# One half of an attention input loaded by a transposing DMA instead of being transposed on TensorE

## The chip, the cores and the metric

The kernel runs on one core of a Trainium2 chip. The core has TensorE (PE, matrix multiply into PSUM), VectorE (DVE), ScalarE (ACT), GpSimd (POOL) and SyncE (SP, which here only issues DMAs). A weight load of TensorE has its own row in the profile (PEld). The metric is device time in microseconds (us) from one execution; the kernel before takes 721.76 us (median of three runs, 721.74 to 721.97).

## The reference

Two independent problems, A and B, of the same shape; the outputs are joined along the last axis. For each, with 16 batches, 80 query rows, width 576, 32 query heads, 16 key/value heads, 512 cached positions and head size 128:

```
q = (x @ wq).reshape(B, Sq, 32, 128).transpose(0, 2, 1, 3)
k, v = repeat(k_cache, 2, axis=1), repeat(v_cache, 2, axis=1)
p = softmax(einsum("bhqd,bhkd->bhqk", q, k) * 128 ** -0.5)
o = einsum("bhqk,bhkd->bhqd", p, v)
out = o.transpose(0, 2, 1, 3).reshape(B, Sq, 4096) @ wo
```

All inputs and the output are bf16.

## The kernel before

**The pieces.** A unit U is one batch and four key/value heads (eight query heads), 64 units a problem, 128 in all. For each unit TensorE makes five score tiles of 128 x 512: four with the first 128 of the 160 query rows of a key head (L673, "S"), and one that gathers the four remainders of 32 rows (L660, "SR", issued for one or two units at a time). On each tile VectorE takes the negated row maximum (L682), ScalarE the exponential with its row sum (L686); VectorE inverts the sums in two groups (L692: tiles 0 to 2, tiles 3 and 4), and GpSimd multiplies the tile by them (L695, "norm"). Then TensorE transposes the five tiles in 40 small matmuls against the identity (L727, "T"), VectorE or ScalarE copies the result to pT (L738 to L747), TensorE multiplies with V (L770, "PV", four matmuls a key head) and VectorE or ScalarE copies to oT (L784). The output projection is L816 ("P", eight matmuls each), with its sums copied at L828 and L845 and stored at L851.

**The query projection** (L537, four matmuls over the first 512 of the 576 columns, "Q", and L550 for the last 64 columns, two matmuls that lie on opposite halves of the array) needs x transposed: `xT[128, half, 5, 640]`, where a half is 8 batches = 640 rows, chunks 0 to 3 hold columns 0 to 511 and chunk 4 holds columns 512 to 575 twice, once in each 64 partitions. Half 0 of problem A is needed first; half 1 from the query projections Q46 on, which stand at about 46 us. There are two ways to fill xT:

- Problem A, both halves: two plain DMAs a half (L375, three and two blocks of 128 rows) into `xs`, which lies in the accumulator `acc`. GpSimd doubles the last 64 columns (L383, two a half). For each block, TensorE does four 128 x 128 transposes into a PSUM bank (L396, "X") and VectorE one copy to xT (L401). For the last columns TensorE does three and two more (L414, "X2"), with two VectorE copies (L418).
- Problem B, both halves: one transposing DMA a half writes chunks 0 to 3 of xT (L431), two small plain DMAs bring the last 64 columns into `xst` (L437, five blocks, and L436, the first block once more), TensorE transposes them in five matmuls (L451, "X2") and VectorE copies in three instructions (L456 to L458).

**Queues.** All DMAs are issued by SP in one order. A K load is a transposing DMA of 1 MB for two units (L626; six slots, so three pairs); a V load is 512 KB for one unit (L630); wo comes in pieces of 576 KB (L590), wq in pieces of 256 KB or 1 MB (L502) with its last 64 rows (L506).

**The order of the work** is written out by hand in a table, `ORDER`. Each operation belongs to a stream; the streams, sorted by name, are given the letters of `LETTERS`. Each letter in the table takes the next operation of its stream; the digits after it are the PSUM banks that it takes; an apostrophe ahead of it sends a copy to ScalarE instead of VectorE. Every engine runs its operations in the order of the table, and the waits follow from it: an operation waits for those whose results it reads and for the readers of what it overwrites. The numbers that are given with each operation (`k_`, `xk`, `XK`) only order operations inside a stream. Some letters: a K loads, h V loads, F wo, K x loads, d query projections, e S, f SR, g T, c PV, b P, j X, k X2, l and m exponentials, o and p maxima, C inverses, u and v norms, M and L the VectorE copies of X and X2.

Read off the table, SP issues at the start (x0 to x3 are the four plain loads of x, K0 is the load for units 0 and 1):

```
x0 x1, wq (12 pieces), K0 x2 K1 x3 V0 V1 K2 wo0 V2 K3 V3 wo1 K4 V4 V5 V6 K5 V7 V8 K6 V9 K7
```

and TensorE, around the transposes of half 1 (X5 to X9 are blocks of four, X22 and X23 the last columns of half 1; Qn with n up to 41 counts L537 groups and L550 pairs):

```
... S8 T0 S9 S10 X5 X6 Q36 X7 S11 Q37 S12 Q38 X22 Q39 X23 S13 PV0 PV1 S14 Q40 Q41 T1
S15 Q42 X8 S16 S17 X9 S18 PV2 PV3 PV4 PV5 SR3 Q43 PV6 PV7 T2 S19 Q44 S20 S21 Q45 T3 ...
```

Of the kernel before, what the change touches and what calls it, by code (L numbers as in the profile page):

```python
# [31 lines left out]
LQ = 12  # L32
QPO = 1
QO = 192
X2K = 6.0
# [8 lines left out]
XK = (15.0, 15.0)  # L44
# [21 lines left out]
omcpg07lCsuc4'yCze1e5'wvmcob7u'Aolue0te2'xe6olhud4hoblholae0Bd5lCove1f23'qolug67Cplud0wumzc1cpu'yc7e2'Axe6smcd
4o'BCg13olutle5uc2xCco'zue7c6'sBd3vlwoe2e4u'ycCod5'Aulhtc1e0huoclag67sloe1'zc2yc'xlCf47Coud6'tBv'wle0pe2c5uAcm
c1ouc'se3od4'tulpg15vlob0'wCyluxe2'zAue1bomhColaue6e7d3oluc5Be2'qocle0d4Colug16sluof57'zvyd2lCpc6u'wc'xp'Ae0uc
1md3Bo'tcmg45hF'se6'yxe1hCBc7u'zFe4oclae5vb3olute0lwboolc7Ce1olud6Acluc4qcCovd3se0ulg25Cou'tf17'yxuCBe4'zd2wvp
lc3d5uAmoe0ucpg16'sulob3wlze4A'ye6bhCouholavc2d1q'xulcd3tme0Bf26og45plpc7mcyd0'wme2sc4oc'ze7d6C'txulBc4cou'Ae5  # L70
c3'socle1g24o'thlChCe7uxb3'who'yua'Ae2le5uoe0b'zuolCe1Bd4ulod6vloc7ue2lCqcc5ovlcg03slCtvf17y'zue2'xCb3p'Buwmpc
6ucAbmuo'sue0le1hoc7ud4'qhold3hae2lcCovg56'tluf01y'zub7w'xCpu'Be2Ambuople0c3oc'qc4'se2d5loce7C'td3vole0ug46lub
2'zCymohb'wJxBGe1'qc7oJcle2hc3Ald4hoe0acClod5vsg16lu'tuf27C'zwyb3u'xpuc6AmcuBe0e1oe4uc5bsloc'qd6tle0od3oe1lg25
olCb4pu'zxmwue0ye5blvABd6oc7ohle1e2Jqd3lGochg04slJof57a'w'yAc1pcb6'tCCx'zvle0d4uo'Be1c2umocd3ule5buloCslug01Cp
'quc2w'x'ye6Aue5cmod4u'zte0d7o'Ble1og23loc6'wCcylud5az'sue2'Ac0xe6lCocuc3'BcCv'toc4e1lcuod7'tlsuf02lg34upmb6y'
zwhpe0'xd3'AaComue1e5c4Blvcoc2c'svod7lute0le4og12ole5bxz'ylCoe0ud2'w'BAc4ule1Cod3v'qhcolc7uhe6Chcloug05h'tsuhl
f17xauB'ye4e6p'wb3'zpmc5od0mocle1Ad7slg24CouCc6'yzvce5'xC'te2wvd4ole6oulboule1Bc5ulAce2oud7'qoc3ulcCsg06lu'tuf
15z'w'ye2pb3'x'Bhomc7hCAculae0e1od4ubplComuc6e0qd2luog35slCuf17x'yBc'wu'zpe0d3'tomc5cCpc6u'Ae2le1scvod4'tvog05
lhuhle6zb2a'yCoume1we0vod5'x'Bc7Aulcoc4cld3t'se6e1log47ole0bCCo'wulzud6'x'yBe1u'Ae7Coc4ld3uo'qe5hvclag02sulof1
4u'wxlAc7cp'yb6p't'ze0e7moe2c5cBlbCouod3lvCc1slue0qcd5omuhhf27tlug46pe0y'wb1'zC'xou'Be6mFbvolue2qc4'Ae5olcac3s  # L80
d1CCpcud4'toulg06vb3'wzluA'xue2me6Bboyld4oe1Fc7od5lhqg02lf36'wz'Ae1xcCoc4u'sce2Blhud7od5'tp'ye1Ke4lob0mCoue2bl
puolvg13lc4z'ycc2q'se1acmoe0e4b3xlCCou'td6Bulwd2ovg15AluCf07w'zCve4'ype5b'AuomFoue1lKc6xd0uKo'qe4lhd3uolcuBc5c
'se2ltg16aob5p'w'zClxuc4ce6u'se2obmCB'Aud4olve0Cc7lod3u'ycug26ltrf17'ywChxve0'zpc5h'AcuDoe2'Be6'sc4oumck3ohuc5
lctd1'sLle0c4d5loe2coalg36C'tud0w'zyue4'xd6'Bolg35AlCpuc2c'yze1vc4'w'xoe3'Ab5umolBe0coc7'te6e1lscCe4oule2baoul
oe0ld3Coud6'sClrug17oluCf45z'yvc2p'wc'xd7uA'tmc1Bucpe2lc3vFoce6mDud4thloe0hg35soe2'zb1o'x'yCwe5luBbColue6lrud3
oDd4luhe0'Ag12holaCf57luyc6z'wvc'x'Ae0pc1'sue2'Bcome6c3pd4lCcCou'td5moug01lsue7z'wc3'xuclBd2ov'Ae1'yd5olg46Ctu
lhf07zhv'ye3pc1'wud4'Aomce2pc6lcod0'shC'xe3tu'Bc1aocle6ub5Cslvome1uc3ocg27u'te3'yzbloe2lrb7ole1e6loe5e3bDolaCC
xlb2uo'Buod6'wluCAd1lruc4g05uf37uy'zc'xwvd5Bpe0bhpmDAc1csd3C'thrumCg46JouDlf12xuwBc7'yczue0e4sc3cpb7'thoGc3ole
6bolCAe0luce5sb4urvoDe7d3ovle6boalome0d5Crlpg14lb7wx'ACov'zc3e6ucoe4'tbu'yomuBc3crhluc5CDe1d7luoclsd2hCvlg36DJ
u'tf04y'w'Aue1'ze5oe7ue3b6Caolupbluomd5xr'Bc1olcd6Cpluc2cvg07tsue2zme1b3Gw'xC'yoJue7oKd4luc0Blcoe2c6'Ascle1oe5  # L90
d0'tolg67oCe2z'xbulov'w'Be1re7'Aud0lCod3ulyKg45uClohuf26Jw'yxKCe1'zupc4hc'ABuc5mae0pcvlc3ocud2ts'sle7d3ome5Cg1
4ovlc6ulxcwod0u'Be7A'yd3o'te1lzg26lCouf45'w'zxd7Aulpe6hc0'yDcoc1'Bacsme2Cc3puclc0ok4umctd6vC'sLe1lug35'toue4'z
e0ob2lo'ye5we1lCbxuBloue6e4'Aoc3lacd7olc5ocld0sC'te1rulg36ovf25'yzue4lpe3b6wmxpc1'Acoh'Bd2mhCCc7svDe0lochud5o'
te1lug47oluCe3xblyuo'zue0e1'wBd4luaod5'Aole7g23rlof06'wz'yc1'xCcp'Auc3le2Bcuc4C'sod5mupe1clue0Coc7mcvhsd2Dot't
ve4lDg67uhlohd3ux'yhze1e0'Bd6o'wlc7oe2lcAc4c'sCoe5ulhg17tulof04v'zCxb2p'wulyd7u'BAmc5pe1cc3msce0ohe6'td5oalg34
olCe1ub'zo'yvxle0wd3CuB'Arc4lucoe2c7uod5le1'scolg06tlCf24zu'yDe7pe1uhb6xamwvCobuplud2Cmrc7uoe0'Ae6c'BuCoc3lcuo
d4lsug15lCtvf07'x'yve6p'wb3'zuBhobuDAlFe1c4moce2e6lod5d0olc1rclDg23t'shpe1'ye6Cwb4umAxuze2'BboCoc7lucc3lsvd5rc
uoe0Dd4thlg67oaf12w'zCCub3'xp'Avyme7e5uobloule1rc6ulcod3Be0lc7Cocud4'tslCg15vhDe7u'zxb6ao'wu'ACyle0e5bpomd3r'B
c7oe1lcoc4'se2d6lCovcg07u'tluf45w'xy'zd1uF'Bpe0luhd7Ac6moucpg23'slc4ze6cob0yle3FbmoaC'tCe2xule6oe5b4uolure3'wb
louolvd2CBe0'Aud6qloug57f14z'x'Bc3y'wc'Ae7d6'sDold3hCplue2c5Ccomug07hplvc1t'xucC'zwe2c5'yuod7'Bcu'se0lthe3uc1o  # L100
ac'Ac5'socme2d6tloe1b4Cloue0lvg35oluby'zxlwe1Ce2uo'Bf35'Aoue0ld6qvFld7phc4ocmc2se1lcpg34htae0y'zb2'xC'w'BuAc3m
ocuc7'sCcolue6e5Cd3olvd4tluoe1g07uCole6vzb'xluo'Be7wud5'qCy'Ae1ulof24ud3plac6ocmg07Cslvpe2'zud6wx'yc1oue7mcAud
0o'te5lBg14olf23zlhc7xchp'Be4c5D'ywe0Ccs'Aud1mohc7uo'tcle2d5sole6g47Coluc0Cz'xuc'yd2ph'wvle7c4oauc'te6'Ac0luoc
b1t'Blse0d4moe7Cg56lovle3uwe0xbo'yuC'zoue7'Ae5qc6lucoc2le1CBcuad3o'slud4olg06tCluf27xCy'ze5ub1'Bpu'womc4ucCe0l
# [162 lines left out]
def bass_concat_heads__gqa_block_cached__gqa_block_cached__near_ridge_kernel(  # L267
# [27 lines left out]
    with ExitStack() as es:  # L295
# [634 lines left out]
```

## Time and profile before

| what | value |
|---|---|
| median of three runs | 721.76 us |
| the profiled execution, its time | 722.56 us |
| its span, first to last instruction | 720.6 us |
| TensorE busy | 715.3 us, 10820 matmuls |
| VectorE, ScalarE, GpSimd busy | 641.3, 639.8, 432.6 us |
| DMA queue of SP | 159.05 MB, 95.6% of 16 engines' span |
| granted TensorE clock | 1.000 |
| x of problem A: plain loads, median to landing | 4.1 us (432 KB), 3.7 us (288 KB) |
| x of problem B: transposing load, median to landing | 7.5 us |
| K loads of problem A: median to landing | 8.9 us |

The page gives busy time by engine, then the chain of work that ended last, then groups of instructions by source line. "Busy" of TensorE is made of intervals whose ends are modelled and that overlap; what one matmul costs in a row of equal ones is the distance between their starts, which the timeline shows. An entry of the waits names the engine that waited and what ended the wait.

### The profile page before, as it was taken

Reading aid. Unit: us, or ns where it says so; the run is one execution under the profiler, and the core shown is the slowest. Engines: PE = TensorE matmul, PEld = TensorE weight load, DVE = VectorE, ACT = ScalarE, POOL = GpSimd, SP = SyncE. Lnnn points to the kernel's source line nnn. Section 1 sums busy time; section 2 is a strip of 40 time slices with the busy share of each in tenths; the row PEclk is TensorE's granted clock in tenths of the full one; section 3 lists DMA queues with packets and bytes.
Section 4 is the critical chain, followed back from the end, with each engine's and each line's share of the span. In section 5 each row is a group of like instructions: output and inputs, shape, how many; then the busy total and the mean of one; then the engine's idle time right before and its main releaser. Section 6 shows DMA issues by size and latency. Waiting matters only on the chain.

```text
span 720.6 us, 26290 instructions
## 1 busy us (share of the span) xinstructions
PE 715.3 (99%) x10820; PEld 513.1 (71%) x10820; DVE 641.3 (89%) x1459; ACT 639.8 (89%) x1844; POOL 432.6 (60%) x650
## 2 busy tenths in 40 slices
PE   9999999999999999999999999999999999999998
PEld 5567767777677777777777777777777777777777
DVE  3999998899888998899998899979999889998995
ACT  1999999799989998789997899989999889998993
POOL 0477755566556675665675567646676656755773
PEclk9999999999999999999999999999999999999999
DMA  9999999899999999999999998999999898988860
GB/s 248 268 269 259 265 255 241 206 189 259 225 241 209 217 254 240 226 254 205 268 207 219 248 245 212 247 236 204 181 262 224 193 241 198 220 194 200 178 199 18
DMA packets 374167, 160.73 MB, mean 223 GB/s; under 512 B 278560, under 2 KB 370976, under 8 KB 374048
## 3 DMA queue, kind: packets, MB, share of 16 engines
q1 hardware_dynamic: 374048, 159.05, 95.6%
q8 instruction: 86, 1.41, 0.8%
q14 instruction: 33, 0.27, 0.1%
HBM read 87.65 MB, written 2.95 MB: 126 GB/s over the span
## 4 chain that ended last, share of the span: by engine, by line
PE 98%; ACT 1%; issue 0%; DVE 0%
PE ps L816 22%; PE ps L770 20%; PE ps L537 19%; PE ps L673 16%; PE ps L727 11%; PE ps L660 5%; PE ps L550 4%; ACT p_sb L686 1%; PE ps L348 0%; PE ps L396 0%; ACT qT L563 0%; PE ps L414 0%; PE ps L451 0%; DVE osb L845 0%; DVE wo_sb L341 0%
## 5 line engine op out<-in xcount | busy, mean ns | idle before, releaser
L695 POOL TENSOR_SCALAR p_sb<-p_sb,rinv 128x512 bf16<-128x512 bf16 x640 | 430.8, 694 | 272.7 <-DVE rinv L692 272.2
L686 ACT ACTIVATE p_sb<-ps,negmax 128x512 bf16<-128x512 f32 x640 | 444.0, 711 | 29.8 <-DVE negmax L682 25.5
L682 DVE TENSOR_REDUCE negmax<-ps 128x1 f32<-128x512 f32 x640 | 419.2, 681 | 27.5 <-PE ps L673 22.2
L770 PE MATMUL ps<-pT,v_sb 128*128 128x160 bf16 x2048 | 191.1, 233 | 0.1
L770 PEld LDWEIGHTS ps<-pT,v_sb 128*128 128x128 bf16 x2048 | 154.0, 98 | 39.5 <-ACT pT L745 3.3
L816 PE MATMUL ps<-wo_sb,oT 128*128 128x288 bf16 x1280 | 181.6, 286 | 0.0
L673 PE MATMUL ps<-kT,qT 128*128 128x512 bf16 x512 | 176.4, 381 | 0.0
L537 PE MATMUL ps<-xT,wq_sb 128*128 128x320 bf16 x1024 | 176.0, 299 | 0.0
L816 PEld LDWEIGHTS ps<-wo_sb,oT 128*128 128x128 bf16 x1280 | 122.1, 98 | 43.2 <-ACT p_sb L686 1.7
L686 ACT ACTIVATION_READ_ACCUMULATOR p_sb<-ps,negmax 128x1 f32 x640 | 144.0, 225 | 0.0
L537 PEld LDWEIGHTS ps<-xT,wq_sb 128*128 128x128 bf16 x1024 | 94.5, 98 | 42.4 <-ACT p_sb L686 2.2
L727 PEld LDWEIGHTS ps<-ident,p_sb 64*128 64x128 bf16 x5120 | 91.4, 95 | 8.8 <-issue 1.1
L727 PE MATMUL ps<-ident,p_sb 64*128 64x64 bf16 x5120 | 96.1, 190 | 1.2 <-ACT qT L563 0.7
L738 ACT COPY pT<-ps 128x512 f32<-128x512 f32 x150 | 88.4, 603 | 9.4 <-PE ps L727 9.0
L740 DVE COPY pT<-ps 128x1024 bf16<-128x1024 bf16 x106 | 72.0, 684 | 13.2 <-PE ps L727 11.7
L563 ACT ACTIVATE qT<-ps 128x320 bf16<-128x320 f32 x131 | 59.5, 462 | 16.2 <-PE ps L550 15.4
L784 DVE CAST oT<-ps 128x320 bf16<-128x320 f32 x129 | 61.5, 482 | 6.5 <-PE ps L770 6.0
L564 DVE TENSOR_SCALAR qT<-ps 128x320 bf16<-128x320 f32 x125 | 59.5, 482 | 8.1 <-PE ps L550 6.6
L673 PEld LDWEIGHTS ps<-kT,qT 128*128 128x128 bf16 x512 | 48.4, 97 | 25.7 <-issue 3.3
L784 ACT CAST oT<-ps 128x320 bf16<-128x320 f32 x127 | 56.4, 448 | 10.2 <-PE ps L770 9.9
L745 ACT COPY pT<-ps 128x128 f32<-128x128 f32 x132 | 36.1, 288 | 7.0 <-PE ps L727 6.8
L692 DVE RECIPROCAL rinv<-rowsum 128x3 f32<-128x3 f32 (+1 forms) x256 | 39.5, 161 | 2.3 <-ACT p_sb L686 2.2
(31 smaller groups left out, 194.7 us busy)
## 6 DMA issues: line engine op xcount, KB each, us to landing
v_sb<-in_A_v_cache_dram SPq DMA_DIRECT2D x64, 512.0 KB, 5.4
v_sb<-in_B_v_cache_dram SPq DMA_DIRECT2D x64, 512.0 KB, 4.9
wo_sb<-in_A_wo_dram SPq DMA_DIRECT2D x8, 576.0 KB, 5.6
wo_sb<-in_B_wo_dram SPq DMA_DIRECT2D x8, 576.0 KB, 5.6
wq_sb<-in_B_wq_dram SPq DMA_DIRECT2D x4, 1024.0 KB, 6.6
out_dram<-osb SPq DMA_DIRECT2D x40, 72.0 KB, 3.4
wq_sb<-in_A_wq_dram SPq DMA_DIRECT2D x8, 256.0 KB, 4.5
wq_sb<-in_A_wq_dram SPq DMA_DIRECT2D x2, 1024.0 KB, 7.3
```

Of the source, the lines that this page charges most:

```text
L537: last = e.matmul(ps[:, vbq[h].phys, QO:QO + 320], lhsT=wq_sb[:, wsl, ck, hi * 128:(hi + 1) * 128], rhs=xT[:, half, ck, n0:n0 + 320], star ...
L563: return e.activation(dst, src, AF.Identity, scale=SCALE)
L673: return e.matmul(ps[:, vb.phys, :], lhsT=qT[:, qsl, bl, gl * 160:gl * 160 + 128], rhs=k_of(U, gl), start=True, stop=True)
L682: return e.tensor_reduce(negmax[:, si:si + 1], ps[:, vb.phys, :], axis=AX.X, op=AluOpType.max, negate=True)
L686: return e.activation(p_sb[:, psl, :], ps[:, vb.phys, :], AF.Exp, bias=negmax[:, si:si + 1], scale=1.0, accum_out=rowsum[:, ss, k:k + 1])
L695: return e.tensor_scalar(p_sb[:, psl, :], p_sb[:, psl, :], rinv[:, ss, k:k + 1], 1.0, op0=AluOpType.mult, op1=AluOpType.mult)
L727: last = e.matmul(dst, lhsT=p_sb[64 * h:64 * h + 64, psls[k_], j * 128:(j + 1) * 128], rhs=ident[64 * h:64 * h + 64, 64 * h:64 * h + 64], ...
L738: return e.copy(pT[:, pts, :, :].bitcast(F32)[:, :, 32 * h:32 * h + 32], ps[:, vtp[h].phys, :].rearrange("p (n c) -> p n c", n=16))
L740: return e.tensor_copy(pT[:, pts, :, 64 * h:64 * h + 64], psb[:, vtp[h].phys, :].rearrange("p (n c) -> p n c", n=16))
L770: last = e.matmul(ps[:, vo.phys, off:off + 160], lhsT=v_sb[:, vs, gl, j * 128:(j + 1) * 128], rhs=pT[:, pts, 4 * gl + j, :], start=(j == 0 ...
L784: return (e.copy if en == "act" else e.tensor_copy)(dst, src)
L816: last = e.matmul(ps[:, vb.phys, 0:DC], lhsT=oT[:, sp_ * (HH // 2) + i, rb * 128:(rb + 1) * 128], rhs=wo_sb[:, 2 * c3 + sp_, i, :], start= ...
```

## The change

Half 1 of problem A is now loaded as the halves of problem B are. The first loop over halves runs over half 0 only; the second runs over three cases (problem, half): (0, 1), (1, 0), (1, 1). The table of the order is made anew; it has 13 operations fewer (two plain x loads, five X and two X2 groups of TensorE, five and two VectorE copies, two GpSimd copies go; three loads, one X2 group and one VectorE operation of three copies come).

```diff
-LETTERS = "abcdefghijklmnopqrstuvwxyzABCDEFGHIJKLMNO"
+LETTERS = "abcdefghijklmnopqrstuvwxyzABCDEFGHIJKLMN"
 ORDER = """
-nEKni7KHHHHHHNj3Ej4IMk5j6MNIj7j3Mk4ILd6Id5IIdd2AaBd1dd5BAd6dd2'Bd1dd6BMd0AdAd7'BAd5Ldd4'A'Bd6dd5'ABKMd7add3'AB
...
+nEKni7KHHHHHINj3j4HMj5k6MNIMk3j4ILd5Id6IIdd2BaAd1dj5Ad6Md2dd4ALd0BBdd3BMd6dd5'B'Ad2dd4BA'Ad6dad3BAd5dd4'ABEf0f
+1pe2e7d3omodle6e5Ad0loe2d4'BphldaCod3vmd6Bu'Aodle1uBd4'Aoe0le7Cd3ouldoe2lf56AC'Boe1ve0ld3puld4pumdouhmAhog2357
+lKCBud6'yze1lud4xo'we7g0235Colvdw'xuz'Be1c2lcouf05'As'ye7Cpe6luc3cpmue2c4ocK'te1mod0Kd3aole5ole7slCCg46ouloud2
+lCc1zv'ye5wue6xloe4cu'Aok7ld0vLh'tuc5lFcoe1Fug67holas'yCe4Buc5'wlCof36u'zcpe1u'te7xo'Bc5vcmAc0ucold2sd3lpe5log
+14Ctle7e0omb5ylod6xe1lCbvo'w'zuBe0lqd7uCoc3cuhg45'shulac3yu'Ad1'zCxcuw'Be0f25'tov'Ae7pe4uld3oumg06ploc2c'zxc7y
...
-        for half in range(NPP):
+        for half in range(1):
             x_ap = probs[0][0]
...
-        for half in range(NPP):
-            x_ap = probs[1][0]
+        for xp, half in ((0, 1), (1, 0), (1, 1)):
+            x_ap = probs[xp][0]
...
-            k_ = 5.0 * (UPR + 16 * half - LQ) - XK[half]
-            S.add("sp", k_, em_ldxt, writes=[R(("xT", half, b_), 1) for b_ in range(NRT)], dsem="d_x%d0" % half,
-                  name="ldxt%d" % half, stream="x")
+            k_ = 5.0 * (UPR * xp + 16 * half - LQ) - XK[half]
+            S.add("sp", k_, em_ldxt, writes=[R(("xT", half, b_), xp) for b_ in range(NRT)], dsem="d_x%d0" % half,
+                  name="ldxt%d.%d" % (xp, half), stream="x")
...
-            S.add("pe", k_ + X2K, em_xtr2, reads=[R(("xst", t), half) for t in range(2)] + [IDENT], writes=[R(vb, 0)],
-                  name="xtt%d" % half, stream="X2", alloc=[vb])
+            S.add("pe", k_ + X2K, em_xtr2, reads=[R(("xst", t), 2 * xp + half) for t in range(2)] + [IDENT], writes=[R(vb, 0)],
+                  name="xtt%d.%d" % (xp, half), stream="X2", alloc=[vb])
```

Read off the new table, SP's order at the start is

```
x0 x1, wq (12 pieces), K0 K1 V0 K2 V1 V2 x2 x3 x4 K3 V3 wo0 wo1 V4 K4 V5 V6 K5 V7 V8 K6 V9 wo2 K7
```

where x2 is the transposing load of half 1 and x3, x4 its two small ones, and TensorE's is

```
... SR0 SR1 S0 S1 Q25 Q26 S2 S3 ... S8 SR2 S9 S10 Q36 Q37 Q38 T0 Q39 S11 Q40 S12 T1 Q41 S13 PV0 PV1 SR3 S14 S15 PV2 PV3
S16 PV4 PV5 S17 Q42 Q43 S18 S19 T2 Q44 PV6 S20 S21 S22 PV7 X22 Q45 PV8 PV9 S23 T3 S24 PV10 SR4 PV11 S25 S26 PV12
PV13 PV14 PV15 Q46 Q47 S27 T4 S28 S29 P0 Q48 ... S32 SR5 S33 S34 Q51 T6 ...
```

where X22 is now the one group of five for the last columns of half 1 (the groups are numbered as they come; it is the third of them). Over the whole table the copies that go to ScalarE change: 68 instead of 56 and 72 instead of 71 of the two oT streams, 27 instead of 23 of the accumulator's, and within five of the old number for the pT and qT copies.

More of the change, by code (lines that the diff above doesn't have):

```diff
@@ L66 @@
[L66 to L80, printed above, removed]
@@ new lines @@
+xe1ob7'tole2FCe5Clobuhohuld3aqule0Cwe1od7v'A'Bof25ulg46pulpb0umw'ye1e2'xombAloe5c3'qcole1c4Cc'sue0'ztd2uold3ol
+g46BCe5'ywuc7hc'Ad4hvlshe1oe2u'xa'zc7CcCo'Bud0ltug36olvf57xlzud1'ypc6u'wc'BCAc3u'scpmd4vCe0'te2muog56oulc3xcu'
+we7lsd0o'yc3c'Be2e5'zob4lAhlte6ac1Ccoue7c3olcubt'sole1d3'qolg56f24'wxlzb7C'ypue1me6uoc5cbCBlhupa'suc3Ame1d5ov'
+qd2olve0Cclug47Co'tuf16lyvb3w'zCup'x'Be0Aubmoupe1lc7ucoh'qc4'se0hd3lohd5hlCe1Gvcog27J'tuJle0uyhb4'xmaoe1we2ob'
+AlCzud3loue0'qc7old6c'Bg14'slf27z'ye5p'xc0'Be1d4wmocc6o'Aclc3td2ple0cC'soug15tue6wmb3Coulze7ub'yov'xlBc5e0'qd2
@@ new lines @@
+loe1e6Clod3ucohlug07aA'se1y'wb4lCou'xc6Be0lubCz'Auoe1cvCd3ltvd5o'qe0lf27g46ppmb1Goh'x'Bc2zJclbay'swmCe0ve2oc4'
+qe7ucCold5utc6le1oucc4'Aoc'sud3lCtug26luf07'yxwuCe1'zpe2d4u'Bpmc3uco'Ad6v'soe0lg35ouluc1yhcld2Jz'te3h'xCe0we1u
+'Bhoc5mchoub6hlsvole7c5c'Ad3thlog04aClue1ze5b'yuCw'xo'Aue0o'qe7c4lvcoc6lue2Bce1old3Csd5'tulog46uolf07z'yb2x'wp
+'Alpc4e6e3'Bocmc1cCCsud5'told4ug01mulue6azb'w'xo'ye1Be7lc3Coe0u'Acod4'quld5ovle2sf16Colug37pub0'zCxauw'Bylbupm
+ve2c7mocc3qe1le6oce0'td5old7Colug12sluhf36z'yvhc0p'xhc'w'Ae1Chc2Amve4ocd5'Butld3ou'sg07Cplue1'ywud2o'ze0c4x'Aa
@@ new lines @@
+234r'zDf17x'ze2'wplb4pme0oe6mc5aCcCyuc1lbouole2vcoe7le3ub0o'tusle1rc6lboolg2457CCruDe3y'wDe0lue2cob5'zuColve1o
+blauColue0rc7'scCu'xlg2356tuof47'zwuc1lpcc6u'xye2mcvoe0'sc3c'toue1lc4ove6hclDb5Ctuh'sCplhug0234ohub'zwyu'xle0r
+vg1234moDf56'zwCc7'xuple1e2ocu'yc4e0Cmpb3uslvobmuolcre1hc7'toe6lDcg2345sloe0c7'ywe1o'zce2lb4tCoule7Cboulxuole0
+c3ruclc6oDe1v'sclg2457tCof36u'yCe0'zCpub5loume7we1uxboluolg0234vrlpc7Duc'wChc5z'yue0c'xCmsug1234o'tuc7'zye6c'w
+ulxc4ocve1'sc3tlcog0257'sc4'zxe6Cycv'wb7'toulbulc3Ccub5suc3g1246cy'zb'txwc3cc4scb6r'trDbDb7brDrD
@@ L437, in em_ldxs @@
                 return e.dma_start(xst[:, 0:NRT, :], src.rearrange("(k p) d -> p k d", p=128))
-            k_ = 5.0 * (UPR + 16 * half - LQ) - XK[half]
-            S.add("sp", k_, em_ldxt, writes=[R(("xT", half, b_), 1) for b_ in range(NRT)], dsem="d_x%d0" % half,
-                  name="ldxt%d" % half, stream="x")
+            k_ = 5.0 * (UPR * xp + 16 * half - LQ) - XK[half]
+            S.add("sp", k_, em_ldxt, writes=[R(("xT", half, b_), xp) for b_ in range(NRT)], dsem="d_x%d0" % half,
+                  name="ldxt%d.%d" % (xp, half), stream="x")
             for t in range(2):
-                S.add("sp", k_ + 0.01 + 0.01 * t, lambda e, t=t, f=em_ldxs: f(e, t), writes=[R(("xst", t), half)], dsem="d_xt",
-                      name="ldxs%d.%d" % (half, t), stream="x")
+                S.add("sp", k_ + 0.01 + 0.01 * t, lambda e, t=t, f=em_ldxs: f(e, t), writes=[R(("xst", t), 2 * xp + half)], dsem="d_xt",
+                      name="ldxs%d.%d.%d" % (xp, half, t), stream="x")
             vb = S.bank()
@@ L458, in em_xev2 @@
                 return e.tensor_copy(xT[64:128, half, 4, 0:128], psb[64:128, vb.phys, NROW - 128:NROW])
-            S.add("pe", k_ + X2K, em_xtr2, reads=[R(("xst", t), half) for t in range(2)] + [IDENT], writes=[R(vb, 0)],
-                  name="xtt%d" % half, stream="X2", alloc=[vb])
-            S.add("dve", k_ + X2K + 0.5, em_xev2, reads=[R(vb, 0)], writes=[R(("xt", half, b_), 1) for b_ in range(NRT)],
-                  name="xte%d" % half, stream="xe2")
+            S.add("pe", k_ + X2K, em_xtr2, reads=[R(("xst", t), 2 * xp + half) for t in range(2)] + [IDENT], writes=[R(vb, 0)],
+                  name="xtt%d.%d" % (xp, half), stream="X2", alloc=[vb])
+            S.add("dve", k_ + X2K + 0.5, em_xev2, reads=[R(vb, 0)], writes=[R(("xt", half, b_), xp) for b_ in range(NRT)],
+                  name="xte%d.%d" % (xp, half), stream="xe2")
         steps = [(g_, b_) for g_ in range(ILV) for b_ in range(8)]
```

98 lines of the change are left out of this document (47 added, 51 removed).

## The prediction

> **What bounds the kernel now.** I read the page first, its busy line and the chain that ended last; then the time by stage, to see whether the bound is the same everywhere; then TensorE's waits and its timeline where the removed transposes stand; last the DMA side. Busy line and chain:
>
> ```profile
> PE 715.3 (99%) x10820; PEld 513.1 (71%) x10820; DVE 641.3 (89%) x1459; ACT 639.8 (89%) x1844; POOL 432.6 (60%) x650
> PE 98%; ACT 1%; issue 0%; DVE 0%
> ```
>
> The chain is nearly all TensorE. By stage (stretch, length, then busy time of PE, PEld, DVE, ACT, POOL, the granted clock, the DMA engines' share, GB/s):
>
> ```profile
> 0.00:20.00 20.00, 18.76 (x125) 10.51 (x126) 7.42 (x20) 3.80 (x7) 1.32 (x8) 1.00 1.05 244
> 20.00:28.00 8.00, 7.52 (x54) 3.30 (x53) 8.00 (x17) 7.99 (x25) 3.38 (x6) 1.00 1.14 278
> 28.00:40.00 12.00, 11.82 (x180) 8.27 (x181) 11.91 (x30) 12.00 (x37) 8.12 (x14) 1.00 1.15 265
> 40.00:60.00 20.00, 20.00 (x353) 13.93 (x351) 19.98 (x47) 20.00 (x62) 14.11 (x22) 1.00 1.11 272
> 60.00:718.00 658.00, 657.24 (x10114) 477.08 (x10111) 593.52 (x1348) 596.05 (x1717) 405.71 (x603) 1.00 0.96 220
> ```
>
> After 60 us PE alone is full; from 20 to 60 us VectorE, ScalarE and the DMA engines are full as well, and this is where the change acts. PE's waits are small, the one at T0 in front:
>
> ```profile
> PE ps L348 <- DVE wo_sb L341: 1.2, 1, 1.2
> PE ps L727 <- ACT qT L563: 0.7, 1, 0.7
> ```
>
> PE's timeline at half 1 of A (start, duration, line, count):
>
> ```profile
> 29.40 0.61 PE L396 MATMUL ps<-ident,acc 128*128 128x128 bf16 x8
> 29.85 0.71 PE L537 MATMUL ps<-xT,wq_sb 128*128 128x320 bf16 x4
> ...
> 32.01 0.34 PE L414 MATMUL ps<-ident,acc 128*128 128x128 bf16 x3
> 32.24 0.72 PE L537 MATMUL ps<-xT,wq_sb 128*128 128x320 bf16 x4
> ```
>
> Eight transposes hold PE from 29.40 to 29.85: 0.45 us, 0.056 us each, though one is recorded at 0.219 us. SP's timeline shows how loaded the DMA side is there:
>
> ```profile
> 22.97 7.11 SPq L626 DMA_TRANSPOSE kT<-in_A_k_cache_dram  x1
> 30.20 0.51 SPq L590 DMA_DIRECT2D wo_sb<-in_A_wo_dram  x1
> 30.75 0.58 SPq L630 DMA_DIRECT2D v_sb<-in_A_v_cache_dram  x1
> 31.38 6.95 SPq L626 DMA_TRANSPOSE kT<-in_A_k_cache_dram  x1
> ```
>
> and the transposing loads of problem B's x, the nearest rows for the new one (shortest, median, longest in ns, then to landing):
>
> ```profile
> L431 SPq DMA_TRANSPOSE xT<-in_B_x_dram x2: 3182/4224/5265, 216.8 to 312.6; - x2
> DMA to landing us min/median/max: 7.3/7.5/7.6
> ```
>
> **TensorE's work.** The removed groups hold PE, by distances to the next start, for 0.45 (X5, X6), 0.26 (X7), 0.22 (X8) and 0.25 us (X9), and the last columns for 0.23 and 0.11: 1.52 us. The five added ones took 0.28 us twice in problem B (238.67 to 238.95, 332.00 to 332.28). Net -1.24. PE is the path there (its only wait near is T0's), so this counts in full. Against it, block 4 of half 0 (X4) stood before the first query projection, while PE waited for VectorE's copies (done at 6.71, Q0 at 6.76); the new order has it behind Q5, in the full stream: +0.22, or 0 if Q0 comes earlier by it.
>
> The TensorE page of the Trainium skill, "TensorE: Matmul & The Clock Gate" (Part 4), gives about 275 ns for such a transpose in a kernel. By that, 20 fewer would be an estimated 5.5 us. The timeline disagrees: 56 ns apart.
>
> **The other engines.** VectorE loses five copies of 0.418 us, one of 0.35 and one of 0.28 (2.72) and gains 0.47, 0.43 and 0.22 (1.11). GpSimd loses two copies, 0.35 and 0.29 us, which stood between the first norms. Neither is on the path, but both lie in the full stretch, ahead of maxima and norms that T0 and T1 wait for. Copies moved to ScalarE: 13 of 0.448 and 4 of 0.415 us, and single ones of 0.29 to 0.60, some 10 us; VectorE gets 11 us lighter. After 60 us ScalarE has 62 us free (596 of 658), which covers it; without that cover it costs up to all 10.
>
> **T0 and T1.** T0 waits 0.66 us now, for the norms of unit 0. In the new order 1.76 us more PE work stands ahead of T0 (counting each group by its distance in the timeline), and 2.25 less ahead of T1. T1 stands at 34.70 now, so it would come at about 34.70 - 0.66 - 2.25 = 31.8; the ten norms it needs end at 32.12 now, and 0.64 earlier without the two copies. The score order changes too: remainder tiles first, so the first inverse needs three exponentials, where it now comes after five; but the second tile group of unit 0 is then queued on GpSimd behind a norm of unit 1. The two waits together: from 0 to 0.7; I take 0.4, near the wait that is there. -0.26.
>
> **Waits that the new order brings.** The table gives each group its bank, so the PE work between the last writer of a bank and its next taker can be counted. A score tile's bank is read by a maximum (0.681) and an exponential (0.711), so it needs at least 1.39; the shortest distance after T1 in the order before is 1.80. In the new order P0 takes bank 5 after S27 with only T4, S28 and S29 between: 0.83 + 2 x 0.216 = 1.26. PV8 comes 1.53 after S20, T6 1.52 after S32. PV12 takes the bank of PV11 after two score tiles, 0.43, where the copy to oT takes 0.448 to 0.482 and the order before never has less than 0.76. PE would stand still for 0.13 to 0.54, 0 to 0.27, 0 to 0.28 and 0.02 to 0.33 us: 0.15 to 1.42. I take 0.8, the middle, as neither bound is nearer to a row. Behind a PE wait everything on PE is late, and there is no gap later to take it up.
>
> **The load.** SP issues three DMAs for two. The plain ones took 0.58 each and stood between K0 and K2; the new ones stand ahead of K3: x2 takes between 3.18 (the shorter in B) and 6.95 us (what K loads of 1.6 times its size take at this stage), x3 and x4 0.6 each. K2 starts at 22.97 - 1.26 - 0.51 = 21.2 (V1 goes behind it); then 7.11, V1 and V2 1.1, x2, 1.2, gaps 0.2: K3 starts at 34.0 to 37.8, now 31.38, and lands 8.9 later, at 42.9 to 46.7. But wo0, 576 KB, has moved behind K3, and 736 KB of x replace 720 KB; if the engines' rate sets the pace, 560 KB less lie ahead and at 265 GB/s K3 lands 2 us sooner than its 40.3 now, at 38.2. K3 is needed first by S24, now behind K3's first user at 45.55, with 1.75 us less PE work ahead: at about 43.6. So its wait is between -5 (none) and 3.1; I take none, since K's issue of 7 us against 3.95 at its shortest says that the engines set the pace, and there is less ahead of them. The small loads x3, x4 land 4.2 (median in B) after an issue at 33 to 37, at 37 to 41.2, and X22 stands at about 41; x2 itself is needed only at Q46, near 46. K4 starts 2.6 to 6.4 later than now, with 3.8 in hand, and is a smaller case of the same.
>
> **Sum.** Span 720.6 - 1.24 + 0.22 - 0.26 + 0.8 = 720.1. The profiled execution took 722.56, 1.96 more than its span, and is 0.80 above the median of the runs; so 722.1 profiled and 721.3 in the runs. Extremes of this case: -1.24 - 0.66 + 0.15 = -1.75, 720.0; and -1.24 + 0.22 + 0.04 + 1.42 = +0.44, 722.2.
>
> **Rivals.**
> - *The gain goes through.* T0 and T1 find their norms ready and the thin banks cost their least: 720.0, faster. For it: 1.11 us more VectorE work and 0.64 of GpSimd's leave the full stretch. Against: that ScalarE is full there too.
> - *K3 comes late (the other side).* The transposing x2 takes as long as a K load, SP's issue sets the pace, and PE stands still at S24 for up to 3.1 us, or at X22 for its small loads: 721.3 + 3.1 = 724.4. It decides if K3 lands over 1.9 us after S24's turn at 43.6. For it: every K load from 9 to 60 us is issued straight after the one before, at 5.5 to 7.6 us each. Against: the smaller queue ahead.
> - *Thin distances all along.* ScalarE's ten more microseconds delay exponentials after 60 us; at 0.03 us for each of 128 units 3.8 us, 725.1. For it: one full stretch shows ScalarE has no room at 20 to 60. Against: 62 us free later.
> - *PE isn't the bound.* PE's intervals overlap, the recorded 99% may hide room, and ScalarE or VectorE paces the stretch from 20 to 60: 1.24 less is worth nothing, 721.8. The Trainium skill's page "Perfetto Trace Analysis" (Identifying the Most-Contended Engine) calls matmul busy a bad measure and wants the weight loads' share, here 71%. Against the rival: PE has one wait of 0.7 after its start.
> - *Transposes at their recorded length.* 20 x 0.219 = 4.4 us less: 717.4; the 56 ns speak against it.
>
> **Chances.** The forecast 0.40, gain goes through 0.20, K3 late 0.20, thin distances 0.10, PE not the bound 0.08, recorded length 0.02. 0.2% is 1.44 us, about what a measurement of this kernel can tell from no change: faster below 720.3, slower above 723.2. Faster 0.22, same 0.48, slower 0.30. The range runs from 719.8, just under the second case, to 724.8, past K3's worst; it leaves out the longest transposes and most of the thin-distance case. The forecast alone: 720.0 to 722.2.
>
> **What would show it.** Right: 25 fewer L396 and L414 and 5 more L451 matmuls between 29 and 42 us, PE full from there, waits of some tenths at P0, PV8, PV12 and T6, K3 landed before 43. Wrong: a PE gap before S24 or X22 that ends with a DMA, idle PE that recurs after 60 us, or a distance between transposes far above 56 ns.

## The result, and the profile after

The changed kernel takes 723.57 us (median of 12 runs, 723.10 to 725.15); the kernel before took 721.61 beside it (12 runs, 720.92 to 722.28). The ratio is 1.0027, with a 95% interval of 1.0020 to 1.0035: slower by 1.96 us, 0.27%. The profiled execution has a span of 721.6 us and a time of 723.31.

The page of the changed kernel, its busy line and the chain that ended last:

```profile
PE 715.8 (99%) x10800; PEld 511.2 (71%) x10800; DVE 632.0 (88%) x1432; ACT 646.4 (90%) x1867; POOL 431.4 (60%) x648
PE 96%; DVE 4%; ACT 0%; issue 0%
```

TensorE has the 20 matmuls less that the change takes away, yet the chain has moved from 98% TensorE to 96%, with 4% on VectorE. Where, the times by stage show (stretch, length, then busy time of PE, PEld, DVE, ACT, POOL, the granted clock, the DMA engines' share, GB/s):

```profile
20.00:28.00 8.00, 8.00 (x59) 3.86 (x55) 8.00 (x18) 7.41 (x23) 2.87 (x5) 1.00 1.12 258
28.00:40.00 12.00, 10.60 (x165) 6.54 (x165) 12.00 (x28) 11.78 (x37) 7.49 (x12) 1.00 1.17 234
40.00:60.00 20.00, 19.50 (x305) 12.73 (x298) 18.34 (x45) 18.32 (x53) 14.42 (x22) 1.00 1.15 274
60.00:718.00 658.00, 657.90 (x10160) 476.94 (x10158) 585.01 (x1323) 605.93 (x1755) 405.34 (x604) 1.00 0.94 221
```

From 28 to 40 us TensorE was busy for 11.82 us before and is for 10.60 now; the removed work, less what is added, is 1.2. In sum nothing moved up into its place: VectorE is busy for the whole 12.00 us, ScalarE for 11.78. After 60 us TensorE is full, as before. The chain followed back through that stretch (start, length, what) lay on ScalarE from 20.01 us to T0 in the kernel before, and on TensorE alone from there to 50 us:

```profile
20.77 3.35 ACT p_sb L686 x10
...
24.45 3.35 ACT p_sb L686 x10
...
28.18 0.76 PE ps L727 x40
```

In the changed kernel it lies on VectorE from 19.87 to 44.96 us, with breaks of 0.03 us at most; its last part:

```profile
35.65 3.58 DVE negmax L682 x6
39.23 0.40 DVE oT L784
...
42.00 1.23 DVE negmax L682 x2
43.23 0.41 DVE xT L456
43.66 0.43 DVE xT L457
44.09 0.14 DVE xT L458
...
44.26 0.70 DVE negmax L682
```

The three xT copies in it are those behind the new group of five transposes, X22. VectorE has not become lighter up to there, though the copies of X5 to X9 have gone. Busy times in us up to 46 us, where S24 stands in both kernels (46.09 and 45.81):

| engine | before | after |
|---|---|---|
| TensorE | 44.10 | 43.03 |
| VectorE | 33.33 | 34.14 |
| ScalarE | 29.79 | 27.73 |

In that time VectorE makes 19 copies to qT and 7 to pT, where it made 17 and 4; ScalarE makes 11 and 6, where it made 15 and 12. The new table thus gives early copies to VectorE that were ScalarE's. No run gives them back alone, so how much of the waits comes from them is not shown. TensorE's waits are now

```profile
PE ps L727 <- DVE qT L564: 0.9, 1, 0.9
PE ps L550 <- DVE oT L784: 0.5, 1, 0.5
PE ps L673 <- ACT p_sb L686: 0.3, 1, 0.3
```

at T0, ahead of T2 and at S24. The list leaves out short ones, and they matter: I took the start of a score tile and subtracted all TensorE groups ahead of it, each at its usual distance to the next start (0.216 for a score tile, 0.277 for four PV matmuls, 0.544 for four projections, 0.69 or 0.825 for a T group, and so on). What is left is time in which TensorE stood. The first two columns also hold some 0.1 us wherever the kind of matmul changes (from a score tile to the next one takes 0.216 us, to a pair of L550 0.312), so only the last column is read here; it can be off by about 0.1 us:

| up to | standing, before | standing, after | more |
|---|---|---|---|
| S0 (19 us) | 2.75 | 3.26 | +0.50 |
| S16 (36 us) | 4.57 | 5.21 | +0.64 |
| S24 (46 us) | 5.12 | 7.14 | +2.02 |
| S30 (53 us) | 5.24 | 8.16 | +2.93 |
| S50 (79 to 82 us) | 6.00 | 9.45 | +3.45 |
| S400 (557 us) | 16.91 | 19.08 | +2.18 |

By S400 the new order has 1.19 us less TensorE work ahead (the forecast said 1.24), and 3.45 us more of standing were there by 80 us. That is +2.3 us, and the runs give +1.96. The column falls again between S50 and S400 because the profiled execution of before stood still three times for 1.24 us in sum at 100, 176 and 185 us, for a reason that is no part of the change (last section); its time of 722.56 lay 0.95 above the median of its runs, which fits.

The loads are not among the waits. SP's queue (start, length, line):

```profile
27.13 4.80 SPq L431 DMA_TRANSPOSE xT<-in_A_x_dram  x1
31.97 0.58 SPq L437 DMA_DIRECT2D xst<-in_A_x_dram  x1
32.60 0.52 SPq L436 DMA_DIRECT2D xst<-in_A_x_dram  x1
33.17 5.39 SPq L626 DMA_TRANSPOSE kT<-in_A_k_cache_dram  x1
```

K3 is issued 1.8 us later than before and lands at 40.5 us, as it did; x2 lands at 36.4 and the small loads at 36.5 and 36.8, six microseconds ahead of X22.

### The profile page after: what moved, and what is told of

Same layout as the page of the kernel before. It is cut to its first block, busy times and chain, and to the rows that moved or that the text cites. A ratio compares the mean times of both kernels' runs of the same rounds, so it can differ in the third digit from the quotient of the medians.

```text
span 721.6 us, 26232 instructions
## 1 busy us (share of the span) xinstructions
PE 715.8 (99%) x10800; PEld 511.2 (71%) x10800; DVE 632.0 (88%) x1432; ACT 646.4 (90%) x1867; POOL 431.4 (60%) x648
## 3 DMA queue, kind: packets, MB, share of 16 engines
q8 instruction: 85, 1.39, 0.8%
## 4 chain that ended last, share of the span: by engine, by line
PE 96%; DVE 4%; ACT 0%; issue 0%
PE ps L816 22%; PE ps L770 20%; PE ps L537 18%; PE ps L673 15%; PE ps L727 10%; PE ps L660 5%; PE ps L550 4%; DVE negmax L682 3%; PE ps L348 0%; DVE qT L564 0%; PE ps L396 0%; DVE pT L740 0%; DVE oT L784 0%; DVE pT L747 0%; ACT p_sb L686 0%; DVE rinv L692 0%
## 5 line engine op out<-in xcount | busy, mean ns | idle before, releaser
L682 DVE TENSOR_REDUCE negmax<-ps 128x1 f32<-128x512 f32 x640 | 419.1, 680 | 36.4 <-PE ps L673 24.1
L673 PE MATMUL ps<-kT,qT 128*128 128x512 bf16 x512 | 178.2, 380 | 0.4 <-ACT p_sb L686 0.3
L816 PEld LDWEIGHTS ps<-wo_sb,oT 128*128 128x128 bf16 x1280 | 121.1, 98 | 44.6 <-ACT p_sb L686 2.1
L686 ACT ACTIVATION_READ_ACCUMULATOR p_sb<-ps,negmax 128x1 f32 x640 | 141.9, 222 | 0.0
L784 ACT CAST oT<-ps 128x320 bf16<-128x320 f32 x140 | 61.0, 440 | 5.7 <-PE ps L770 4.9
L564 DVE TENSOR_SCALAR qT<-ps 128x320 bf16<-128x320 f32 x121 | 57.6, 480 | 7.0 <-PE ps L550 6.3
L784 DVE CAST oT<-ps 128x320 bf16<-128x320 f32 x116 | 55.4, 479 | 5.3 <-PE ps L770 4.6
L747 DVE COPY pT<-ps 128x256 bf16<-128x256 bf16 x123 | 33.5, 281 | 8.3 <-PE ps L727 7.4
```

The costliest lines, as they stand in the source:

```text
L673: return e.matmul(ps[:, vb.phys, :], lhsT=qT[:, qsl, bl, gl * 160:gl * 160 + 128], rhs=k_of(U, gl), start=True, stop=True)
L682: return e.tensor_reduce(negmax[:, si:si + 1], ps[:, vb.phys, :], axis=AX.X, op=AluOpType.max, negate=True)
L686: return e.activation(p_sb[:, psl, :], ps[:, vb.phys, :], AF.Exp, bias=negmax[:, si:si + 1], scale=1.0, accum_out=rowsum[:, ss, k:k + 1])
L784: return (e.copy if en == "act" else e.tensor_copy)(dst, src)
L816: last = e.matmul(ps[:, vb.phys, 0:DC], lhsT=oT[:, sp_ * (HH // 2) + i, rb * 128:(rb + 1) * 128], rhs=wo_sb[:, 2 * c3 + sp_, i, :], start= ...
```

## The experiments

Three theories. *Order*: the new table sets the time, by waits of its own, and with the old order the gain would come. *Hidden*: in the full stretch TensorE's work was never worth its length, because VectorE and ScalarE are at their limit with it. *Load*: the transposing DMA delays what stands behind it. Beside the runs' times I compare stretches inside the profiles: kernels with the same order repeat each other there to a few hundredths of a microsecond where the edit does not act (from S0 to T0 the nine profiles of the old order take 8.82 to 8.84 us), while times of whole runs carry some 0.5 us of other things. There is one profiled execution of each kernel. The stretch used most runs from the start of T0 to the start of P0 (the first output group), 21.70 us before. The two rows of TensorE's timeline in the kernel before:

```profile
28.18 0.76 PE L727 MATMUL ps<-ident,p_sb 64*128 64x64 bf16 x40 [0.66 <-ACT qT L563]
49.88 1.14 PE L816 MATMUL ps<-wo_sb,oT 128*128 128x288 bf16 x8
```

### Is it the load?

**e3_plain_load**: the changed kernel, where x of half 1 comes by a plain DMA of the same bytes into the same place; the transposing is left out, so x is not in its transposed form there.

```diff
+                if x_ap is probs[0][0]:
+                    return e.dma_start(xT[:, half, 0:4, :]..., src[:, 0:512].rearrange("(k p) d -> p k d", p=128))
                 return e.dma_start_transpose(xT[:, half, 0:4, :], src[:, 0:512].rearrange("n (c d) -> n c d", c=4))
```

> The kernel after with a plain DMA of the same 640 KB in place of the transposing one (x of half 1 of A is not transposed, so its projections are of other data). Theories 'order' and 'hidden': no change against the kernel after, 723.6 within 0.4. Rival 'load' in the form that transposing is what costs: back to 722 or less.

Measured: 723.74 us, ratio to before 1.0027 (1.0016 to 1.0039), the same as the change. From S0 to S36 both lose the same 1.75 us against before. The transposing kind of the DMA costs the kernel nothing here. The Trainium skill's page "Advanced Engine Details and Errata" (X-Bar Transpose (TRN2)) says that such DMAs are as fast as regular ones. The traces do not agree for this one: its 640 KB land 9.2 us after the issue with the transposing and 6.6 us without. The run times can't tell, since x2 lands at 36.4 us and its first reader, Q46, starts at 49.2.

**e8_extra_load**: the kernel before with the transposing load added right behind K2, into space nobody reads then.

```diff
+        S.add("sp", 6.0, em_extra, writes=[R(("V", 4), -1), R(("V", 5), -1)], dsem="d_xt", name="extra", stream="zz")
```

> The kernel before with the new transposing load of 640 KB added right behind K2, into two V slots that are still empty; nothing reads it, TensorE and VectorE do all that they did. Theories 'order' and 'hidden': K3 lands 4 to 5 us later, with 5.2 in hand, K4 and K5 alike: no change or a few tenths more, 721.6 to 722.2. Rival 'load': the loss of the change comes back, 723 or more.

Measured: 723.71 us, 1.0026 (1.0013 to 1.0039). K3 lands at 46.0 instead of 40.4, and TensorE waits for DMAs:

```profile
PE ps L667 <- DMA kT<-in_A_k_cache_dram: 0.6, 1, 0.6
PE ps L777 <- DMA v_sb<-in_A_v_cache_dram: 0.4, 1, 0.4
```

So a load more in this stretch does cost, as *load* expected (723 or more). The change doesn't pay that: K3 lands when it did. It also takes two plain x loads away and issues wo0 behind K3 instead of ahead of it; which of these makes the room was not tried alone.

### What is TensorE's work worth there?

**e5_60_more_transposes** and **e6_15_fewer_transposes**: the kernel before with X5 to X9 at 16 transposes instead of four, and at one. In e6 the copies spread the one result over all four places, so three quarters of half 1's transposes are left out.

```diff
-                        for ck in range(4):
+                        for ck in list(range(4)) * (4 if rb >= NRT else 1):     # e5
+                        for ck in range(4 if rb < NRT else 1):                  # e6
```

> The kernel before with every transposing group X5 to X9 issued four times over into the same bank: 60 more 128 x 128 transposes between 29 and 37 us, nothing else changed. If TensorE is the path there and one costs 56 ns: 3.4 us more, 725.0. If VectorE and ScalarE pace that stretch (theory 'hidden'): well under 2 us more. If a transpose costs its recorded 219 ns: 13 us more, 734.7.

> The kernel before with one transpose instead of four in each of X5 to X9 (15 fewer; the copy behind them keeps its size and writes that one chunk four times, so three quarters of the first 512 columns of x, half 1 of A, are left out). If TensorE is the path there: 15 x 56 ns = 0.84 less, 720.8. Theory 'hidden' (VectorE and ScalarE run at the same pace, so TensorE gains nothing by having less): no change, 721.6 within 0.3.

Measured: e5 725.84 us, 1.0055 (1.0043 to 1.0067); e6 722.34 us, 1.0008 (0.9999 to 1.0016). The two rows of e6:

```profile
28.54 0.76 PE L730 MATMUL ps<-ident,p_sb 64*128 64x64 bf16 x40 [0.66 <-ACT qT L566]
50.21 1.14 PE L819 MATMUL ps<-wo_sb,oT 128*128 128x288 bf16 x8
```

From T0 to P0 e6 takes 21.67 us, 0.03 less than before, with 0.84 us less TensorE work in it (15 at 56 ns). e5 takes 24.80, 3.10 more, or 52 ns for each transpose added. Work added to TensorE counts nearly in full, work removed counts for nothing. *Hidden*, as it was put for e5 (well under 2 us more), missed by far: TensorE has hardly any room in this stretch. For e6 it had no change within 0.3, and the interval says no gain. A bound that TensorE holds alone gives back what it takes; this one doesn't.

**e1_oldorder_newload**: the old order with the new load. X5 to X8, X22 and X23 and their copies go, X9's place takes the new group of five, and on SP the three x loads stand ahead of K3.

Read off the tables:

```diff
-SP:  ... K0 x2 K1 x3 V0 V1 K2 wo0 V2 K3 V3 wo1        (x2, x3: plain loads)
+SP:  ... K0 K1 V0 K2 V1 x2 x3 x4 V2 K3 V3 wo0 wo1
-PE:  X5 X6 X7 X8 X22 X9 X23, each at its place
+PE:  X22 (five transposes) at X9's place
```

> The order of the kernel before, with the new load of half 1 of A and nothing else new: X5 to X8, X22, X23 and their copies go, the one group for the last columns stands where X9 stood, and the x loads stand ahead of K3. Theory 'order' (the loss is made by the new table, which puts other work on VectorE in the stretch from 20 to 45 us, and the load itself pays): about 1 us less than the kernel before, 720.6. Theory 'hidden' (VectorE and ScalarE pace 20 to 45 us whatever the table, so TensorE's saved 1.24 us are waited away): 721.6, within 0.4 of the kernel before. Rival 'load' (the transposing load, its small loads or the three copies behind it make the loss): 723 or more.

Measured: 724.02 us, 1.0032 (1.0020 to 1.0043). The old order does not bring the gain either: from T0 to P0 it takes 0.48 us more than before with 1.24 less to do. The list of its waits names no DMA. TensorE's timeline shows waits where the X groups had stood:

```profile
29.91 0.72 PE L537 MATMUL ps<-xT,wq_sb 128*128 128x320 bf16 x4 [0.16 <-DVE pT L740]
30.84 0.39 PE L673 MATMUL ps<-kT,qT 128*128 128x512 bf16 x1 [0.21 <-ACT pT L738]
40.18 0.73 PE L770 MATMUL ps<-pT,v_sb 128*128 128x160 bf16 x8 [0.17 <-ACT p_sb L686]
```

*Order* as the only cause is out. But *hidden* had 721.6 within 0.4 here, and only *load* had 723 or more. Part of *load* were the three copies behind the new group, and e1's chain does lie on VectorE from 36.82 to 39.32 us, with these three (37.52 to 38.59) between two maxima. From 28 to 40 us none of the three engines is full in e1 (TensorE 11.21, VectorE 11.15, ScalarE 11.60 of 12), so full engines alone don't explain it; what the copies cost in the old order was not tried. The rest of e1's 2.4 us is not in this stretch; its profile has a further 1.2 us of the stalls of the last section, and I don't account for all of it.

### Are VectorE and ScalarE at their limit as well?

**e10_copies_twice** gives VectorE five copies more (1.7 us), **e13_three_more_exp** ScalarE three exponentials (1.7 us by their distances to the next start, 0.57 to 0.59 each), in the order and with the loads of before.

```diff
+                        if half:                                                             # e10
+                            e.tensor_copy(xs[:, half * NRT + blk, 0:512], psb[:, vb.phys, 0:512])
...
+                    if U == 2 and 1 <= k <= 3:                                               # e13
+                        e.activation(v_sb[:, 5, k, :], ps[:, vb.phys, :], AF.Exp, ...)
```

> The kernel before with a second VectorE copy of each of the five banks X5 to X9 (five more of about 0.4 us, 0.34 between starts, between 30 and 38 us). If VectorE is at the limit in that stretch as theory 'hidden' says: about 1.7 us more, 723.3. If only TensorE limits it: no change, 721.6.

> The kernel before with three more exponentials on ScalarE in the third unit of scores (each about 0.65 us, some 2 us in all, at about 30 us), whose output nobody reads. Theory 'hidden' (ScalarE is at its limit in that stretch as TensorE and VectorE are) expects most of it in the time: 722.6 to 723.6 us, with TensorE waiting behind ScalarE. Rival: ScalarE has room there, since the page shows it at 90 percent over the span, and the time stays at 721.3 to 721.9 us.

Measured: e10 722.84 us, 1.0017 (1.0008 to 1.0025); e13 723.21 us, 1.0018 (1.0009 to 1.0026). From T0 to P0 e10 takes 23.19 us, 1.49 of its 1.7 more; e13 23.43, 1.73 more, which is all of its 1.7. In e10 TensorE now waits for VectorE's copies:

```profile
PE ps L539 <- DVE xT L403: 0.4, 1, 0.4
```

So each of the three engines, loaded further, lengthens the stretch by nearly all of it, though the page shows VectorE and ScalarE at 89% over the span.

**e11_pe_and_dve_lighter** and **e14_all_three_lighter** turn this round. e11 is before with one transpose and a quarter of the copy in X5 to X9; e14 has in addition four exponentials of the third unit cut to 128 of 512 columns. What is left out is filled with zeros at the start.

```diff
+                        if half:                                                             # e11, e14
+                            return e.tensor_copy(xT[:, half, 0, blk * 128:(blk + 1) * 128], psb[:, vb.phys, 0:128])
...
+                    if U == 2 and 1 <= k <= 4:                                               # e14
+                        return e.activation(p_sb[:, psl, 0:128], ps[:, vb.phys, 0:128], AF.Exp, ...)
```

> The kernel before with the X groups of the second half of the first problem's x (X5 to X9) cut to one transpose each and their five VectorE copies cut to a quarter; it leaves out three quarters of that half of x (those rows of xT are filled with zeros by GpSimd at the start), so its time says what lighter work is worth and nothing else. TensorE has about 0.8 us less (15 transposes of 56 ns), VectorE about 1.2 us less, in the same order and with the same loads. Taking the 15 transposes alone away gave 722.34 us, no gain. Theory 'hidden' says that the stretch from 28 to 45 us is held by TensorE, VectorE and ScalarE together, so that ScalarE, full from 28 to 40 us, keeps most of the time: 721.0 to 721.9 us, and ScalarE still at 11.8 us or more of those 12. Rival: VectorE was the only thing behind TensorE, so with both lighter the gain of about 0.8 us comes through: 720.4 to 720.9 us, with TensorE above 11.6 of 12 us there.

> The kernel with the lighter X groups and copies (the second half of the first problem's x cut to a quarter, TensorE about 0.8 us and VectorE about 1.2 us less) and, new, the four exponentials of the third unit over 128 of their 512 columns, so that ScalarE has about 1.2 us less at 26 to 34 us as well; the other columns of P are filled with zeros by GpSimd at the start and are left out of the result. The lighter TensorE and VectorE alone gave 721.93 us, no gain, with ScalarE busy for all of 28 to 40 us. Theory 'hidden' (the three engines are full there together, and work comes off the time only when it comes off all three) expects the gain to appear now: 720.6 to 721.1 us, 0.5 to 1.0 below the kernel before. Rival: something else paces this stretch (distances of banks, GpSimd's normalisations, loads) and lighter engines bring nothing: 721.4 to 721.9 us.

Measured: e11 721.93 us, 1.0001 (0.9992 to 1.0010), no gain, at the upper end of what *hidden* had for it. e14 721.60 us, 0.9996 (0.9987 to 1.0005): the expected gain of 0.5 to 1.0 is not seen in the runs, whose median lies where the rival had it; they can't tell 0.5 us from none. The stretch can. Busy times from 28 to 40 us, in e11 and then in e14:

```profile
28.00:40.00 12.00, 11.83 (x170) 7.41 (x166) 11.56 (x31) 12.00 (x38) 8.23 (x13) 1.00 1.15 259
```

```profile
28.00:40.00 12.00, 11.97 (x196) 7.76 (x190) 11.77 (x33) 11.42 (x38) 8.59 (x14) 1.00 1.17 255
```

and the rows of T0 and P0 in e14:

```profile
27.83 0.76 PE L738 MATMUL ps<-ident,p_sb 64*128 64x64 bf16 x40 [0.65 <-ACT qT L571]
49.06 1.14 PE L827 MATMUL ps<-wo_sb,oT 128*128 128x288 bf16 x8
```

| kernel | work changed (us) | T0 to P0 | against before |
|---|---|---|---|
| before | | 21.70 | |
| e6 | TensorE -0.84 | 21.67 | -0.03 |
| e11 | TensorE -0.84, VectorE -1.0 | 21.65 | -0.05 |
| e14 | TensorE -0.84, VectorE -1.0, ScalarE -1.2 | 21.23 | -0.47 |
| e10 | VectorE +1.7 | 23.19 | +1.49 |
| e13 | ScalarE +1.7 | 23.43 | +1.73 |
| e5 | TensorE +3.4 | 24.80 | +3.10 |

(VectorE's five copies are recorded at 0.418 us each in before and at 0.215 in e11.) Only the kernel in which all three are lighter gets shorter. What e14 has beyond e11 is the lighter ScalarE, and no run lightens ScalarE alone, or it and TensorE without VectorE. So the runs show that ScalarE has to be lighter for a gain; that the others must be as well is not shown. e14 gets 0.47 of about 0.84; ScalarE now stands behind VectorE, as its timeline shows:

```profile
32.67 0.69 ACT L697 ACTIVATE p_sb<-ps,negmax 128x512 bf16<-128x512 f32 x1 [0.55 <-DVE negmax L690]
```

The profiled execution of e14 lost the gain again in one stall at 69 us (last section).

### What makes the waits of the new order?

**e2_oev_earlier** puts one oT copy of VectorE, for which TensorE stands ahead of T2, two maxima earlier. **e12_after_short_xcopy** keeps only the smallest of the three copies behind X22 (VectorE -0.85 us; the rest of that strip of x is zeros). **e4_xcopies_on_act** gives all three to ScalarE. The lines of e2 are read off the tables.

```diff
-VectorE: ... max14 max15 ... max17 oT1                                                      # e2
+VectorE: ... max14 max15 oT1 ... max17
...
+                if not xp:                                                                   # e12
+                    return e.tensor_copy(xT[64:128, half, 4, 0:128], psb[64:128, vb.phys, NROW - 128:NROW])
...
-            S.add("dve", k_ + X2K + 0.5, em_xev2, ...                                        # e4
+            S.add("dve" if xp else "act", k_ + X2K + 0.5, em_xev2, ...
```

> The kernel after with one VectorE copy to oT (of unit 1, the one T2 waits 0.45 and 0.63 us around) moved ahead of two maxima. Theories 'order' and 'hidden': T2 starts up to 0.6 us sooner, but two maxima come 0.4 later, so 0 to 0.5 us less than the kernel after: 723.1 to 723.6. Rival 'load': no change, 723.6.

> The changed kernel with only the last and smallest of the three VectorE copies behind the transposes of the first problem's second half (64 partitions by 128 columns); it leaves out the rest of that strip of x, which GpSimd fills with zeros at the start. VectorE has about 0.85 us less at about 43 to 44 us, and nothing else moves. Theory 'order' (the new table's waits have VectorE on the chain up to 45 us) expects 722.7 to 723.3 us, the waits ahead of T3, S24 and PV10 shorter by about as much in sum. If those waits come from elsewhere (ScalarE, or the distances of banks alone), the time stays at that of the change, 723.4 to 723.8 us.

> The kernel after with the three copies of the last columns of half 1 of A on ScalarE instead of VectorE (1.07 us of VectorE at 43.2 to 44.2 us). Theories 'order' and 'hidden': VectorE's chain from 19.9 to 45 us is 1 us shorter and ScalarE has 1.7 us idle between 40 and 60, so 0.4 to 1.0 us less, 722.6 to 723.2. Rival 'load': no change.

Measured: e2 723.15 us, 1.0024 (1.0016 to 1.0033); e12 723.26 us, 1.0024 (1.0015 to 1.0033); e4 724.82 us, 1.0040 (1.0027 to 1.0053). The first two came within what was expected of them, yet the intervals overlap with the change's, and the traces don't bear the gains out. In e2 the wait ahead of T2 falls from 0.63 to 0.45 us, and by T3 nothing of it is left; in e12 S24 comes 0.31 earlier, and of that 0.12 is left at S36. e4 missed: the three copies take ScalarE from 43.12 to 44.6 us, ahead of a copy to oT, and by the profile TensorE stands ahead of S23 for that copy:

```profile
PE ps L674 <- ACT oT L785: 1.0, 1, 1.0
```

From S0 to S36 e4 loses 2.99 us against before where the change loses 1.75. So none of the single copies tried holds the new order back. Which change of the table would keep TensorE's 1.2 us is open. None of the kernels tried was shown to be faster than the one before.

## Why the prediction was wrong

The range, 719.8 to 724.8, held the 723.57. The forecast of 721.3 was 2.3 too low, on the other side of before.

- **TensorE's work.** The size was right: 1.24 forecast, 1.19 by the order's own groups, and 56 ns for a transpose stands (52 added inside the stretch in e5; by the runs 70, with stalls in it). The step that failed is the sentence "PE is the path there (its only wait near is T0's), so this counts in full". Before the change, the few waits of TensorE in this stretch meant that TensorE was *just* as long as VectorE and ScalarE, not that it was the longest. e6 and e11 took 0.84 away for a gain of 0.03 and 0.05. The row that said so was in the text, 12.00 of 12 for ScalarE and 11.91 for VectorE from 28 to 40 us, and was read as cover instead of as a bound. The chain in the kernel before lies on TensorE alone from 28.18 to 50 us, and yet its work was worth nothing: a chain names what came last, and not by how little.
- **The rival that PE isn't the bound** had this mechanism and its price (721.8; e11 gave 721.93, e6 722.34), but a chance of 0.08. The Trainium skill's page "Perfetto Trace Analysis" (Identifying the Most-Contended Engine) asks for the one most-contended engine and its improvement first. In this stretch no engine stands out: TensorE, VectorE and ScalarE are busy for 11.82, 11.91 and 12.00 of 12 us.
- **Waits that the new order brings.** The second failure, in size: 0.8 taken, 1.42 at most, and 3.45 measured, which includes T0's and the 0.50 ahead of S0. The places that were named came about as bounded (P0 0.13, T6 0.13, PV12 0.24; at PV8 nothing above 0.13). What was missing are mostly the waits between S16 and S30: 0.63 ahead of T2, 0.33 ahead of S24, 0.27 ahead of S29, 0.21 ahead of T3, 0.18 each ahead of S20 and X22 (the figures at T2, T3 and T6 hold 0.10 for the change of the kind of matmul). Bank distances count only TensorE work between two takers; they don't show that the copy or the maximum in between is itself late. That these are late because VectorE's queue is full is what the chain suggests up to 45 us; no run shows it.
- **T0 and T1.** 0.26 of gain forecast. T0's wait grew from 0.83 to 0.97 by distances between starts, and T1 came at 32.90 where 31.8 was worked out: no gain. T1 moving up by 1.8 us on its own is the order, not time won.
- **X4 in the stream.** +0.22 forecast; from Q0 to S0 the five profiles of the new order take 0.3 to 0.5 more.
- **The other engines.** "Neither is on the path" was wrong for VectorE in the stretch: e10 shows 1.49 of 1.7 us coming through. The copies that change engines were counted over the whole table, where VectorE did get lighter (641.3 to 632.0 us); up to 46 us it got 0.81 heavier. The first rival, too, has 1.11 us of VectorE's work leaving the full stretch, where 2.72 less 1.11 is 1.61. For the time after 60 us the cover held: TensorE is full there, 657.90 of 658.
- **The load.** Right. K3 came at 40.5 (38.2 to 46.7 forecast, no wait taken), the small loads at 36.5 and 36.8 (37 to 41.2 forecast), x2's issue took 4.80 (3.18 to 6.95). *K3 comes late* did not happen; e8, where the load comes on top of the others, shows how that looks (K3 at 46.0, 1.0 us of waits). *Thin distances all along* did not either, and the *recorded length* is out by e5.

## What to carry to other kernels

Where two or three engines are full in the same stretch, work taken from one of them can be worth nothing (0.03 of 0.84 us here) while work added to any of them costs nearly its length; "this engine hardly waits" doesn't tell it from its neighbours, so compare the busy times of all engines in that stretch before counting a saving. Here a gain showed only when ScalarE was lighter as well. Count work that changes engines by stretch too, and not only over the whole kernel. Compare landmarks inside two profiles as well as whole runs: for kernels of one order they repeat to hundredths of a microsecond, far finer than the medians.

## What had not been expected of the hardware

TensorE sometimes stops in the middle of a group of equal matmuls for 0.3 to 1.4 us, with nothing to wait for. In e14 a group of 40 transposes breaks off after 36, and in e3 another after 35; the rest comes later, as in e14's timeline:

```profile
69.09 0.23 PE L738 MATMUL ps<-ident,p_sb 64*128 64x64 bf16 x4 [0.89 <-issue]
```

"Issue" means that the profile shows no releaser. The places differ: before at 100, 176 and 185 us (1.24 in sum), e1 at 96 us (1.1), e8 at 67 and 144 us (0.56 and 0.73), the change and e10 none of that size. Where TensorE's matmuls are the same, the place can be the same as well: before and e13 both stop after 34 of T14's 40 transposes and after 19 of T29's, e6 and e14 both after 36 of T8's; e10, with the matmuls of before, stops at neither. Just ahead of those that I looked at, by up to 3 us, stands a transfer of the instruction queue, of which the page counts 85 in the change (1.39 MB), while the DMA engines are over 90% busy with the kernel's own loads. That instructions come late behind data is therefore likely, but no run here tried it. It means that differences of about 1 us between whole runs of different programs can come from places that the edit never touched.
